# Attention scores from unsplit float32, each head of a pair in its own 64 rows of the array

## The chip, the cores and the metric

One core of a Trainium2 chip runs the whole program in one launch. The metric is the device time of that core in microseconds (us); smaller is better. TensorE (PE) multiplies matrices, and its weight loads (PEld) are shown as an engine of their own; VectorE is DVE, ScalarE is ACT, GpSimd is POOL, and SyncE (SP) issues all the transfers.

## The reference

Only the first part, the attention with its memory term, is touched. The two mixture and feed-forward parts behind it take the attention's output and stay as they are.

```python
B, H, S, D = (4, 8, 576, 64)          # q, k, v are (B, H, S, D) in float32
scores = (1 / np.sqrt(D)) * np.matmul(q, k.transpose(0, 1, 3, 2))
scores = np.where(np.triu(np.ones((S, S), bool), k=1), -1e9, scores)
a = np.exp(scores - scores.max(-1, keepdims=True))
a /= a.sum(-1, keepdims=True) + 1e-09
local = np.matmul(a, v)
...                                   # q_p = phi(q); mem_out = (q_p @ M_prev) / (q_p . z_prev)
out = g * mem_out + (1 - g) * local   # g = sigmoid(beta), one number for each head
```

## The kernel before

The 32 heads are worked in 16 pairs. A pair has 576 queries, cut into tiles t = 0 to 3 of 128 and a last tile of 64; in the last tile both heads share one array of 128 rows. Because of the causal mask, tile t needs 128(t + 1) keys and the last tile all 576, in two halves of 288 columns.

Scores are made from split numbers. `split` takes a head's queries and keys (both copies of them lie in the 128 partitions of `raw`) and writes the operands into one of three buffers R: part 0 writes the values rounded to the type float32r, part 1 the rests of the queries (in partitions 64 to 127), part 2 the rests of the keys. `scores` then multiplies twice over all 128 rows of the array, L361 with the keys' high parts and L362 with their rests, and adds up in PSUM. In the steady state the three parts run on POOL (L311, L331, L333). `scores_last` does the same for the last tile with four products for each half (L375, L376).

After a product, DVE scales it, adds the mask and finds the row's extreme (L363, or L378 for the last tile), and ACT takes the exponentials (L366, L384). The weights are transposed on PE (L401, L409) and copied to SBUF into PT by ACT or DVE (L251, L253), multiplied by the values (L454, L456, L461, the two heads in their own 64 columns of the array), transposed back (L477), combined with the memory term (L423 and L438) and transposed once more for the slots' logits (L501, L508, L515).

`step(p)` writes one pipeline step: scores of pair p + 1, transposes of pair p, values of pair p - 1, and the slots' softmax once in four pairs. Each piece has a position from the table T, the pieces are sorted by it, and that order is the priority in which a scheduler places the instructions in each engine's queue; an engine then runs its queue in order. Pieces of other work lie in the steps too: the decoding of the float64 weights `win` (ACT L230, DVE L233 to L236), the features of the memory term (L341, L345, L347), and one load of expert weights for each step.

PSUM has two banks for scores (pool pS), three for transposes (pT; combine, x_transposes and logits use it as well), and three others. PT exists once, the queries with values and memory (Q) twice. When attention ends, its buffers are filled with expert weights in the order of `places`: raw64, R2, raw, F, R0, R1, Q0, Q1, PT, M, P, x.

Of the kernel before, what the change touches and what calls it, by code (L numbers as in the profile page):

```python
# [8 lines left out]
F32 = mybir.dt.float32  # L9
# [17 lines left out]
# columns of the constants  # L27
# [6 lines left out]
# columns of the operands of the scores: 64 zeros, queries, 64 zeros, keys, keys' rests; the last 64  # L34
# queries come last for a pair's first head and first for its second
A_Q = 64
A_K1 = 704
A_K2 = A_K1 + S
A_END = A_K2 + S

# columns of a pair's second load: queries, values, memory with its norm
# [7 lines left out]
# a float64's high word read as a float32 grows with its size: at float32's smallest exponent, and  # L49
# at the largest value that float32 has  # L50
# [9 lines left out]
    load64=0.12317024323385276,  # L60
# [3 lines left out]
    val=[-0.023467514121727075, -0.010343477991731534, 0.01420002951651116, 0.08623092642954787, 0.17749026616632413],  # L64
    vout=0.1962084482935497,
# [19 lines left out]
    ps=0,  # L85
# [9 lines left out]
    s0=['a', 'm', 'p', 'v'],  # L95
# [11 lines left out]
ORDERS = [  # L107
# [8 lines left out]
]  # L116


CHOICES = {"NB": [3, 4], "sim": [0, 1]}
# [8 lines left out]
def tile_attention_moe_ffn(  # L128
# [37 lines left out]
    SIZE = {  # L166
        "raw": 2 * 2 * S, "R0": A_END, "R1": A_END, "R2": A_END, "P": 3200, "Q0": M_END, "Q1": M_END, "PT": 2 * 1984,
# [12 lines left out]
    # in the order they are used: 512 columns of w1 (expert group, row block, expert, half) and of w2  # L180
# [5 lines left out]
    def load_place(n, tag):  # L186
        """The next n units of weights, in a place of that many."""
# [78 lines left out]
    R = [place(f"R{i}", A_END, F32R) for i in range(3)]  # L266
# [25 lines left out]
    for i in range(3):  # L292
        POOL.memset(R[i][:, 0:64].bitcast(F32), 0.0)
        POOL.memset(R[i][:, 640:704].bitcast(F32), 0.0)
# [3 lines left out]
    raw_t, qvm_t, x_t, st_t, y_t, o_t, u_t = {}, {}, {}, {}, {}, {}, {}  # L298
# [16 lines left out]

    def split(p, h, part, eng=None):
        """Query and key rows as the high parts of their values, then the rests: the operands
        [q_hi; q_lo] and [k_hi; k_hi], [k_lo; k_lo]."""
        r, raw = R[(2 * p + h) % 3], raw_t[p, h]
        q = slice(A_Q, A_Q + S)  # L320
        if part == 0:
            dst = strided(r[:, A_Q:A_Q + 1], (A_K1 - A_Q, 2), (1, S))
            src = strided(raw[:, 0:1], (S, 2), (1, S))
            if eng in (None, "p"):
                pool_copy(dst, src)
            elif eng == "v":
                DVE.tensor_copy(dst, src)
            else:
                ACT.activation(out=dst, in_=src, func=AF.Copy)  # L329
        elif part == 1:  # L330
            (DVE if eng in ("a", "v", "m") else POOL).tensor_tensor(out=r[64:128, q], in0=raw[64:128, 0:S], in1=r[64:128, q], op=ALU.subtract)  # L331
        else:
            (DVE if eng in ("a", "v", "n") else POOL).tensor_tensor(out=r[:, A_K2:A_END], in0=raw[:, S:2 * S], in1=r[:, A_K1:A_K2], op=ALU.subtract)  # L333
            load_qk(p + 1, h)
# [14 lines left out]
    def stats(p):  # L349
        """0..7: sums (t, h), 8..17: norms (t, h), 18..25: minus the maxima, 26, 27: the last tile's."""  # L350
# [4 lines left out]
    def scores(p, h, t):  # L355
        r, st, pt = R[(2 * p + h) % 3], stats(p), Pt[h, t]
        n, c = 128 * (t + 1), 2 * t + h
        ps = pS.tile([128, 512], F32, tag="s", name="s")
        o = A_Q + 64 * h + t * 128
        a = r[:, o:o + 128]  # L360
# [248 lines left out]
    def step(p):  # L609
# [5 lines left out]
        if 1 <= p + 1 < NPAIR:  # L615
            add(T["rest"], load_rest, p + 1)
# [377 lines left out]
```

## Time and profile before

| | us |
|---|---|
| median of 3 runs | 591.15 |
| lowest, highest | 590.99, 593.15 |
| profiled execution, span from first to last instruction | 590.7 |
| PE busy in it | 548.4 (93%), with 3095 matmul instructions |
| DVE busy | 421.1 (71%) |
| ACT busy | 292.0 (49%) |
| POOL busy | 253.8 (43%) |

The profiled execution has only its span to show; the median of the runs lies 0.45 us above it, within their scatter. The span falls into the attention's start (to about 31 us), its steady steps (30.9 to 263.3), its end (to 290.5), the experts (to 345) and the last two layers (to 590.7). A matmul's row lasts from its start to the modelled end of its pipeline, so that rows overlap and a busy PE is not one at its peak: the pace of PE is read from the distance of successive rows.

### The profile page before, as it was taken

The numbers are of one execution on the slowest core, as the hardware profiler recorded it, in microseconds if no ns is written. First come the engines' busy times: TensorE is split into PE (matmuls) and PEld (weight loads), VectorE is DVE, ScalarE is ACT, GpSimd is POOL, SyncE is SP. The second block draws the span as 40 slices with busy tenths as digits, with TensorE's granted clock in tenths as the row PEclk, the third lists the DMA queues.
The fourth block names the chain that finished last, engine by engine and source line by source line (L and its number), as shares of the span: only waits on it lengthen the run. The fifth ranks groups of instructions, "written<-read, shape, count | busy, mean of one in ns | idle before, by whom it ended". The sixth has DMA issues, their size and how long they took to land.

```text
span 590.7 us, 9038 instructions
## 1 busy us (share of the span) xinstructions
PE 548.4 (93%) x3095; PEld 381.7 (65%) x3095; DVE 421.1 (71%) x978; ACT 292.0 (49%) x757; POOL 253.8 (43%) x234
## 2 busy tenths in 40 slices
PE   3899999989989999999999978878999999999997
PEld 2666665757646766666533235656888888888886
DVE  5889999998989999884324089997447557474670
ACT  4676767566656766663122065545463241423322
POOL 4486566763546667310000027899641140412302
PEclk9999999998989999999999999989999999999999
DMA  7667666543543545276899644240002010000101
GB/s 259 223 239 277 240 244 255 208 166 98 191 161 113 173 139 166 97 266 202 299 368 386 232 144 143 72 143 0 1 32 77 0 54 1 26 30 1 53 1 53
DMA packets 28957, 86.14 MB, mean 146 GB/s; under 512 B 3056, under 2 KB 3184, under 8 KB 28912
## 3 DMA queue, kind: packets, MB, share of 16 engines
q1 hardware_dynamic: 28912, 85.58, 40.8%
q8 instruction: 24, 0.39, 0.3%
q14 instruction: 21, 0.17, 0.1%
HBM read 80.85 MB, written 4.72 MB: 145 GB/s over the span
## 4 chain that ended last, share of the span: by engine, by line
PE 70%; DVE 17%; POOL 6%; issue 4%; ACT 2%; DMA 1%; SPq 0%; POOLq 0%; ACTq 0%; DVEq 0%
PE y L909 10%; PE y L907 10%; PE y L908 10%; PE t L401 5%; PE o L461 4%; PE y L770 3%; DVE P L363 3%; PE s L361 3%; POOL P L889 3%; PE o L456 3%; PE y L754 3%; PE h L878 2%; PE s L362 2%; POOL R L314 2%; PE y L423 2%
## 5 line engine op out<-in xcount | busy, mean ns | idle before, releaser
L909 PE MATMUL y<-w,R 128*128 128x512 f32 x288 | 115.5, 402 | 5.4 <-POOL R L314 5.4
L889 POOL TENSOR_SCALAR P<-P,sbt 128x384 f32<-128x384 f32 x31 | 34.8, 1122 | 198.3 <-ACT P L884 198.3
L907 PE MATMUL y<-w,R 128*128 128x512 f32 x288 | 115.6, 401 | 3.1 <-POOL R L311 2.9
L908 PE MATMUL y<-w,R 128*128 128x512 f32 x288 | 114.6, 398 | 1.4 <-DVE w L867 1.4
L882 ACT ACTIVATE P<-h 128x384 f32<-128x384 f32 x96 | 47.2, 491 | 121.6 <-PE h L878 121.3
L366 ACT ACTIVATE P<-P,st 128x128 f32<-128x128 f32 (+3 forms) x128 | 71.3, 559 | 32.6 <-DVE st L363 32.1
L893 DVE SCALAR_TENSOR_TENSOR P<-P,sbt 128x384 f32<-128x384 f32 x58 | 45.3, 781 | 56.1 <-ACT P L882 56.1
L363 DVE CUSTOM_DVE_ANT_0 P<-s,cs 128x128 f32<-128x128 f32 (+3 forms) x128 | 60.2, 481 | 13.7 <-PE s L362 13.5
L909 PEld LDWEIGHTS y<-w,R 128*128 128x128 f32 x288 | 55.0, 191 | 21.7 <-POOL R L314 8.3
L907 PEld LDWEIGHTS y<-w,R 128*128 128x128 f32 x288 | 55.1, 191 | 18.0 <-POOL R L311 5.6
L251 ACT ACTIVATE PT<-t 128x512 f32<-128x512 f32 (+3 forms) x144 | 55.9, 413 | 21.2 <-PE t L401 15.1
L908 PEld LDWEIGHTS y<-w,R 128*128 128x128 f32 x288 | 55.1, 191 | 11.4 <-DVE w L867 1.7
L361 PE MATMUL s<-R 128*128 128x128 f32 (+3 forms) x128 | 52.6, 413 | 10.3 <-DVE R L331 6.3
L401 PE MATMUL t<-cs,P 128*128 128x128 f32 x320 | 61.2, 296 | 0.2
L311 POOL TENSOR_SCALAR R<-raw 128x1152 fp32r<-128x1152 f32 x29 | 35.5, 1225 | 47.4 <-PE s L376 29.0
L401 PEld LDWEIGHTS t<-cs,P 128*128 128x128 f32 x320 | 38.4, 145 | 24.1 <-issue 13.1
L461 PE MATMUL o<-PT,Q 128*64 128x192 f32 (+3 forms) x256 | 52.0, 400 | 0.0
L333 POOL TENSOR_TENSOR R<-raw,R 128x576 fp32r<-128x576 f32 x30 | 45.8, 1528 | 8.8 <-ACT R L329 6.9
L331 POOL TENSOR_TENSOR R<-raw,R 64x576 fp32r<-64x576 f32 x29 | 45.1, 1556 | 2.4
L314 POOL TENSOR_TENSOR R<-P,R 128x384 fp32r<-128x384 f32 x38 | 44.3, 1165 | 3.2
L362 PE MATMUL s<-R 128*128 128x128 f32 (+3 forms) x128 | 43.1, 339 | 0.0
L895 DVE SCALAR_TENSOR_TENSOR R<-P,sbt,R 128x384 fp32r<-128x384 f32 x58 | 37.6, 649 | 5.4
(230 smaller groups left out, 1037.4 us busy)
## 6 DMA issues: line engine op xcount, KB each, us to landing
raw<-in_qk_dram SPq DMA_DIRECT2D x32, 576.0 KB, 3.7
Q<-in_qvm_dram SPq DMA_DIRECT2D x16, 673.0 KB, 5.0
w<-in_w_dram SPq DMA_DIRECT2D x19, 512.0 KB, 5.9
raw<-in_w_in_dram SPq DMA_DIRECT2D x8, 1024.0 KB, 5.7
w<-in_w_dram SPq DMA_DIRECT2D x32, 256.0 KB, 5.4
out_dram<-P SPq DMA_DIRECT2D x18, 256.0 KB, 2.1
raw<-in_w_out_dram SPq DMA_DIRECT2D x4, 1024.0 KB, 4.7
R<-in_w_dram SPq DMA_DIRECT2D x6, 512.0 KB, 6.1
```

What stands on the lines that cost most here:

```text
L251: ACT.activation(out=dst, in_=src, func=AF.Copy)
L314: POOL.tensor_tensor(out=dst, in0=a, in1=b, op=ALU.subtract)
L361: PE.matmul(ps[:, 0:n], a, r[:, A_K1:A_K1 + n], start=True, stop=False)
L362: PE.matmul(ps[:, 0:n], a, r[:, A_K2:A_K2 + n], start=False, stop=True)
L363: DVE.tensor_tensor_reduce(out=pt, in0=ps[:, 0:n], in1=cs[:, C_M2 - n:C_M2], scale=-0.125, scalar=BIG, op0=ALU.add, op1=ALU.min, accum_out ...
L366: ACT.activation(out=pt, in_=pt, func=AF.Exp, scale=-1.0, bias=st[:, 18 + c:19 + c], accum_out=st[:, c:c + 1])
L401: PE.transpose(tp[:, kb * 128:(kb + 1) * 128], Pt[h, t][:, kb * 128:(kb + 1) * 128], ident)
L461: last_pe[0] = PE.matmul(o[64 * h:64 * h + 64, q0 - 64:512], lhs(h), PT[p][0:rows, h, c:c + S - q0], start=False, stop=(kb == 4))
L889: POOL.tensor_scalar(out=r, in0=r, scalar1=sbt[:, 0:1], scalar2=sbt[:, 1:2], op0=ALU.mult, op1=ALU.add)
L907: PE.matmul(acc[g, i], hi[:, c], who[k], start=(k == 0), stop=False)
L908: PE.matmul(acc[g, i], hi[:, c], wlo[k], start=False, stop=False)
L909: PE.matmul(acc[g, i], lo[:, c], who[k], start=False, stop=(k == NK - 1))
```

## The change

Queries and keys are no longer split. A score is one float32 product over 64 rows of the array: the pair's first head uses rows 0 to 63, its second head rows 64 to 127, each with a PSUM bank of its own; in the last tile the two heads write the two halves of one bank. The keys are loaded alone (two loads of 64 partitions for each pair) into two halves of R1, the queries come from the pair's other load Q, of which there are now three (R2 is the third). `split` with its loads and the clearing of R is gone. PT exists twice (the second one in raw and R0). The tiles come in one order, 0, 1, last, 2, 3, each with transposes of both heads and then scores of both heads; the tables of offsets for them are gone. The values of a step have one position (0.05) instead of five. The pools change to three banks for scores and two for transposes (`ps=1`). Comments and docstrings are gone, and with them nothing that runs.

```diff
-    rest=0.695170733550659,
-    split=[-0.04277104398158898, 0.03196566297869962, 0.3161963354764645, 0.5106726172649579, 0.6789307619040896, 0.9898536413841046],
+    rest=0.35,
+    keys=0.02,
...
-    tpos=[-0.007428014231922566, -0.007428014231922566, -0.0017186653760416053, -0.007428014231922566, -0.007428014231922566, 0.2502093330615674, 0.0044618983662577764, -0.007428014231922566, -0.059387670387742744, -0.029043334600072676],
-    spos=[0.0023645466460246217, 0.0023645466460246217, 0.0023645466460246217, 0.14689391857384748, 0.0023645466460246217, -0.00397236720777216, 0.03582678126241105, 0.0023645466460246217, -0.0450101998423876, 0.0040102512909126285],
-    order=4,
...
-    val=[-0.023467514121727075, -0.010343477991731534, 0.01420002951651116, 0.08623092642954787, 0.17749026616632413],
-    vout=0.1962084482935497,
+    val=[0.05, 0.05, 0.05, 0.05, 0.05],
+    vout=0.08,
...
-    ps=0,
+    ps=1,
...
+ORDER = [0, 1, 4, 2, 3]
...
-    R = [place(f"R{i}", A_END, F32R) for i in range(3)]
+    KA = place("R1", SIZE["R1"])
...
-    PT = [place("PT", SIZE["PT"]).rearrange("p (h c) -> p h c", h=2)] * NPAIR
-    QA = [place(f"Q{i}", M_END) for i in range(2)]
-    raws = place("raw", SIZE["raw"])
+    PTA = place("PT", SIZE["PT"])
+    PT = [[PTA[:, 0:1984], PTA[:, 1984:3968]], [place("raw", SIZE["raw"])[:, 0:1984], place("R0", SIZE["R0"])[:, 0:1984]]]
+    QA = [place("Q0", M_END), place("Q1", M_END), place("R2", SIZE["R2"])[:, 0:M_END]]
...
-    def load_qk(p, h):
+    def load_keys(p):
         if p < NPAIR:
-            raw_t[p, h] = raws[:, 2 * S * h:2 * S * h + 2 * S]
-            SP.dma_start(out=raw_t[p, h], in_=qk[2 * p + h])
+            k_t[p] = KA[:, S * (p % 2):S * (p % 2) + S]
+            for h in range(2):
+                r = slice(64 * h, 64 * h + 64)
+                SP.dma_start(out=k_t[p][r, :], in_=qk[2 * p + h, r, S:2 * S])
...
-            qvm_t[p] = QA[p % 2]
+            qvm_t[p] = QA[p % 3]
...
-    def split(p, h, part, eng=None):
...
-        r, st, pt = R[(2 * p + h) % 3], stats(p), Pt[h, t]
+        st, pt, r = stats(p), Pt[h, t], slice(64 * h, 64 * h + 64)
...
-        PE.matmul(ps[:, 0:n], a, r[:, A_K1:A_K1 + n], start=True, stop=False)
-        PE.matmul(ps[:, 0:n], a, r[:, A_K2:A_K2 + n], start=False, stop=True)
+        PE.matmul(ps[:, 0:n], qvm_t[p][r, t * 128:(t + 1) * 128], k_t[p][r, 0:n], start=True, stop=True)
...
         for h in range(2):
-            r = R[(2 * p + h) % 3]
-            a = r[:, 0:128] if h else r[:, A_Q + 512:A_Q + 640]
-            k = 288 * g
-            PE.matmul(ps[:, 0:288], a, r[:, A_K1 + k:A_K1 + k + 288], start=(h == 0), stop=False)
-            PE.matmul(ps[:, 0:288], a, r[:, A_K2 + k:A_K2 + k + 288], start=False, stop=(h == 1))
+            r = slice(64 * h, 64 * h + 64)
+            PE.matmul(ps[r, 0:288], qvm_t[p][r, 512:S], k_t[p][r, k:k + 288], start=True, stop=True)
...
-        if 1 <= p + 1 < NPAIR:
-            add(T["rest"], load_rest, p + 1)
+        if p >= 0:
+            add(T["rest"], load_rest, p + 2)
+            add(T["keys"], load_keys, p + 2)
...
-        if 0 <= p + 2 < NPAIR:
-            for h in range(2):
-                for part in range(3):
-                    add(T["split"][3 * h + part], split, p + 2, h, part, T["s0"][2 + h] if p < 0 else None)
...
+        for t in ORDER:
             pos = acc / tot
...
+            acc += 6 if t == 4 else 2 * t + 2
             if 0 <= p < NPAIR:
...
+                if t == 4:
+                    add(T["scl"], scale_last, p)
+                for i in range(2):
+                    if t < 4:
+                        add(pos, transposes, p, i, t)
+                    else:
+                        add(pos, transposes_last, p, i)
             if 0 <= p + 1 < NPAIR:
...
+                for i in range(2):
+                    if t < 4:
+                        add(pos + 0.001, scores, p + 1, i, t)
+                    else:
+                        add(pos + 0.001, scores_last, p + 1, i)
...
-    load_qk(0, 0)
+    load_keys(0)
+    load_rest(0)
     SP.dma_start(out=cs, in_=cst)
-    load_qk(0, 1)
     SP.dma_start(out=bet, in_=beta)
-    load_rest(0)
+    load_keys(1)
+    load_rest(1)
...
-    for h in range(2):
-        for part in range(3):
-            split(0, h, part, T["s0"][h])
```

## Rows read from the trace of the kernel before

**Rows 1.** Busy time by stretch; the engines' columns are named in the first line
```profile
core 0: us, PE busy (x) PEld busy (x) DVE busy (x) ACT busy (x) POOL busy (x), PEclk, DMA share, GB/s
...
30.90:263.30 232.40, 220.33 (x1488) 148.98 (x1487) 214.04 (x602) 155.08 (x472) 133.28 (x101) 0.98 0.54 189
```

**Rows 2.** The chain of waits, 30.9 to 263.3 us, shares by line
```profile
by line: PE t L401 11.9%; PE o L461 7.5%; DVE P L363 6.4%; PE s L361 6.3%; PE o L456 5.4%; PE s L362 5.2%; PE y L423 4.8%; DVE win L235 4.1%; DVE F L347 3.6%; DVE win L234 3.4%; PE t L501 3.0%; DVE win L236 3.0%; DVE win L233 2.7%; issue 2.
```

**Rows 3.** PE in order of time, one step: start us, duration us, what
```profile
154.07 0.29 PE L375 MATMUL s<-R 128*128 128x288 f32 x1
...
154.21 0.30 PE L376 MATMUL s<-R 128*128 128x288 f32 x1
...
155.20 0.63 PE L501 MATMUL t<-cs,x 128*128 128x128 f32 x4 [0.43 <-DVE x L494]
...
155.76 0.27 PE L508 MATMUL t<-cs,x 64*128 64x64 f32 x1
...
155.96 0.66 PE L401 MATMUL t<-cs,P 128*128 128x128 f32 x4
...
156.69 0.40 PE L362 MATMUL s<-R 128*128 128x512 f32 x1
...
156.93 0.49 PE L401 MATMUL t<-cs,P 128*128 128x128 f32 x3
```

**Rows 4.** The same view, float32 products of the values
```profile
159.98 1.07 PE L456 MATMUL o<-PT,Q 128*64 128x512 f32 x2
...
161.42 0.64 PE L456 MATMUL o<-PT,Q 128*64 128x512 f32 x1
...
164.05 0.76 PE L461 MATMUL o<-PT,Q 128*64 128x320 f32 x4
```

**Rows 5.** Groups of POOL's instructions, 30.9 to 263.3 us: busy us, mean ns
```profile
L331 POOL TENSOR_TENSOR R<-raw,R 64x576 fp32r<-64x576 f32 x27 | 42.3, 1566 | 2.2
...
L311 POOL TENSOR_SCALAR R<-raw 128x1152 fp32r<-128x1152 f32 x26 | 32.1, 1233 | 46.4 <-PE s L376 29.0 <-PE s L362 17.4
```

**Rows 6.** DVE and POOL in order of time, in one step
```profile
162.95 1.15 POOL L311 TENSOR_SCALAR R<-raw 128x1152 fp32r<-128x1152 f32 x1 [3.64 <-PE s L362]
...
163.11 1.59 DVE L347 SCALAR_TENSOR_TENSOR F<-Q,F 128x576 f32<-128x576 f32 x1
```

**Rows 7.** Groups of DVE's instructions, 30.9 to 263.3 us: busy us, mean ns
```profile
L347 DVE SCALAR_TENSOR_TENSOR F<-Q,F 128x576 f32<-128x576 f32 x13 | 16.5, 1268 | 0.0
L235 DVE SCALAR_TENSOR_TENSOR win<-raw,win 128x512 int32<-128x512 int32 x16 | 16.1, 1007 | 0.0
L234 DVE TENSOR_SCALAR win<-win 128x512 int32<-128x512 int32 x16 | 15.6, 982 | 0.1
```

**Rows 8.** The same three lines: shortest, median and longest duration, ns
```profile
L347 DVE SCALAR_TENSOR_TENSOR F<-Q,F x13: 739/1234/1971, 48.7 to 248.9; 128x576 f32<-128x576 f32 x13
...
L235 DVE SCALAR_TENSOR_TENSOR win<-raw,win x16: 678/690/1920, 37.3 to 254.5; 128x512 int32<-128x512 int32 x16
...
L234 DVE TENSOR_SCALAR win<-win x16: 412/1028/1656, 35.4 to 253.8; 128x512 int32<-128x512 int32 x16
```

**Rows 9.** PE in order of time, the start of the program
```profile
6.33 0.79 PE L361 MATMUL s<-R 128*128 128x128 f32 x2 [6.33 <-DVE R L331]
...
14.35 0.44 PE L375 MATMUL s<-R 128*128 128x288 f32 x1
14.59 0.44 PE L376 MATMUL s<-R 128*128 128x288 f32 x1
...
20.07 0.28 PE L362 MATMUL s<-R 128*128 128x128 f32 x1
```

**Rows 10.** Groups of ACT's copies out of PSUM, 30.9 to 263.3 us: busy us, mean ns
```profile
L251 ACT ACTIVATE PT<-t 128x384 f32<-128x384 f32 x42 | 20.2, 482 | 6.7 <-PE t L401 4.3 <-PE t L409 2.3
```

**Rows 11.** SP and PE in order of time, the end of the attention
```profile
277.43 2.46 SPq L199 DMA_DIRECT2D PT<-in_w_dram  x4
...
290.54 1.92 PE L754 MATMUL y<-w,slT 128*32 128x512 f32 x16 [0.47 <-DVE slT L740]
```

More of the change, by code (lines that the diff above doesn't have):

```diff
@@ L32 @@
 C_END = C_REP + 128
[L36 to L39, printed above, removed]
+A_END = 1984
 M_V = S
@@ L94 @@
     dsum2=0.5750298499964066,
-    s0=['a', 'm', 'p', 'v'],
     cp=['pppddppppppqpqqq', 'dpdpppdpqdqddddq', 'pddpddddddddddpp'],
@@ L104 @@
 )
-ORDERS = [
[8 rows of a table removed]
-]
-CHOICES = {"NB": [3, 4], "sim": [0, 1]}
+ORDER = [0, 1, 4, 2, 3]
 def strided(ap, *dims):
@@ L166, in tile_attention_moe_ffn @@
     SIZE = {
-        "raw": 2 * 2 * S, "R0": A_END, "R1": A_END, "R2": A_END, "P": 3200, "Q0": M_END, "Q1": M_END, "PT": 2 * 1984,
+        "raw": 2 * 2 * S, "R0": A_END, "R1": 1856, "R2": 1856, "P": 3200, "Q0": M_END, "Q1": M_END, "PT": 2 * 1984,
         "raw64": 2048, "F": 1280, "x": 2560, "M": 1280}
@@ L291, in tile_attention_moe_ffn @@
         POOL.memset(FI[i][:, S:640], 0.0)
-    for i in range(3):
-        POOL.memset(R[i][:, 0:64].bitcast(F32), 0.0)
-        POOL.memset(R[i][:, 640:704].bitcast(F32), 0.0)
     POOL.memset(lT, NEG)
     POOL.memset(lgs, 0.0)
-    raw_t, qvm_t, x_t, st_t, y_t, o_t, u_t = {}, {}, {}, {}, {}, {}, {}
-    def load_qk(p, h):
+    k_t, qvm_t, x_t, st_t, y_t, o_t, u_t = {}, {}, {}, {}, {}, {}, {}
+    def load_keys(p):
         if p < NPAIR:
-            raw_t[p, h] = raws[:, 2 * S * h:2 * S * h + 2 * S]
-            SP.dma_start(out=raw_t[p, h], in_=qk[2 * p + h])
+            k_t[p] = KA[:, S * (p % 2):S * (p % 2) + S]
+            for h in range(2):
+                r = slice(64 * h, 64 * h + 64)
+                SP.dma_start(out=k_t[p][r, :], in_=qk[2 * p + h, r, S:2 * S])
     def load_rest(p):
         if p < NPAIR:
-            qvm_t[p] = QA[p % 2]
+            qvm_t[p] = QA[p % 3]
             SP.dma_start(out=qvm_t[p], in_=qvm[p])
@@ L314, in pool_sub @@
         POOL.tensor_tensor(out=dst, in0=a, in1=b, op=ALU.subtract)
-    def split(p, h, part, eng=None):
[L319 to L334, printed above, removed]
     def feature(p, part):
@@ L401, in transposes @@
             PE.transpose(tp[:, kb * 128:(kb + 1) * 128], Pt[h, t][:, kb * 128:(kb + 1) * 128], ident)
-        evac(strided(PT[p][:, h, 128 * t:128 * t + 1], (448, t + 1), (1, 128)),
+        evac(strided(PT[p % 2][h][:, 128 * t:128 * t + 1], (448, t + 1), (1, 128)),
              strided(tp[:, 0:1], (128, t + 1), (1, 128)), T["pt"][(4 * h + t) % len(T["pt"])])
@@ L409, in transposes_last @@
             PE.transpose(tp[:, i * 128:(i + 1) * 128], PL[:, (k0 + i) * 128:(k0 + i + 1) * 128], ident)
-        evac(strided(PT[p][:, 0, 448 * k0 + 512:448 * k0 + 513], (64 if k0 else 448, n), (1984, 2), (1, 64)),
-             strided(tp[:, 0:1], (128, n), (64, 2), (1, 64)), T["ptl"][part % len(T["ptl"])])
+        for h in range(2):
+            evac(strided(PT[p % 2][h][:, 448 * k0 + 512:448 * k0 + 513], (64 if k0 else 448, n), (1, 64)),
+                 strided(tp[:, 64 * h:64 * h + 1], (128, n), (1, 64)), T["ptl"][h])
     def memory(p, part):
@@ L453, in values @@
             for h in range(2):
-                PE.matmul(y[64 * h:64 * h + 64, 260:324], lhs(h), PT[p][:, h, 0:64], start=True, stop=True)
+                PE.matmul(y[64 * h:64 * h + 64, 260:324], lhs(h), PT[p % 2][h][:, 0:64], start=True, stop=True)
             for h in range(2):
-                PE.matmul(o[64 * h:64 * h + 64, :], lhs(h), PT[p][:, h, 64:576], start=True, stop=False)
+                PE.matmul(o[64 * h:64 * h + 64, :], lhs(h), PT[p % 2][h][:, 64:576], start=True, stop=False)
             return
@@ L460, in values @@
             c = 448 * kb + q0 if kb < 4 else 1920
-            last_pe[0] = PE.matmul(o[64 * h:64 * h + 64, q0 - 64:512], lhs(h), PT[p][0:rows, h, c:c + S - q0], start=False, stop=(kb == 4))
+            last_pe[0] = PE.matmul(o[64 * h:64 * h + 64, q0 - 64:512], lhs(h), PT[p % 2][h][0:rows, c:c + S - q0], start=False, stop=(kb == 4))
     def values_out(p):
@@ L626, in step @@
                 add(T["feat"][part], feature, p + 1, part)
-        order = ORDERS[T["order"]]
-        cost = [3 if h == 2 else t + 1 for h, t in order]
-        tot = float(sum(cost))
+        tot = float(sum(6 if t == 4 else 2 * t + 2 for t in ORDER))
         acc = 0.0
-        for n, ((h, t), c) in enumerate(zip(order, cost)):
+        for t in ORDER:
             pos = acc / tot
-            acc += c
+            acc += 6 if t == 4 else 2 * t + 2
             if 0 <= p < NPAIR:
-                if h < 2:
-                    add(pos + T["tpos"][n], transposes, p, h, t)
-                elif t == 0:
-                    add(pos + T["scl"], scale_last, p)
-                    add(pos + T["tpos"][n], transposes_last, p, 0)
-                    add(pos + T["tpos"][n], transposes_last, p, 1)
-            if 0 <= p + 1 < NPAIR:
-                if h < 2:
-                    add(pos + T["spos"][n] + 0.001, scores, p + 1, h, t)
-                else:
-                    add(pos + T["spos"][n] + 0.001, scores_last, p + 1, t)
+                if t == 4:
[5 more added lines that the diff above has]
+                        add(pos, transposes_last, p, i)
+            if 0 <= p + 1 < NPAIR:
+                for i in range(2):
[3 more added lines that the diff above has]
+                        add(pos + 0.001, scores_last, p + 1, i)
         for i in range(16):
@@ L820, in tile_attention_moe_ffn @@
     layer2(1)
-    RC = [place(f"R{i}", A_END, F32R) for i in range(3)]
+    RC = [place(f"R{i}", SIZE[f"R{i}"], F32R) for i in range(3)]
     ring = [RC[i][:, 1024 + TG * j:1024 + TG * j + TG] for i in range(2) for j in range(2)]
```

4 lines of the change are left out of this document (1 added, 3 removed), and 8 rows, old and new, of the table ORDERS.

## Prediction, before the result was known

> **What bounds the kernel now.** I read the table of stretches first, to find where the change can act: the steady steps of the attention take 232.4 us, which is 14 steps of 16.6 us, and there PE and DVE both look full (220 and 214 us) while POOL is at 133 [rows 1]. Neither number says which of them sets the step, so the chain of waits comes second [rows 2]. The lines listed there are PE's for 44% of the stretch (L401, L461, L361, L456, L362, L423, L501) and DVE's for 23% (L363, L235, L347, L234, L236, L233): two parts PE to one part DVE, and POOL has no line among them. Third I read PE in order of time for the pace of each kind of product, because a row's duration contains its pipeline and only the distance of rows is its cost [rows 3, 4]. Last I asked why a decode or a feature, which are SBUF work of fixed size, can take up to four times its shortest duration [rows 6 to 8].
>
> **The scores on PE.** A float32r product of 512 columns is followed by the next work 0.24 us later (156.69 to 156.93), one of 288 columns 0.14 us later, and 128 columns of a transpose cost 0.11 us (four in 0.63, a single one being 0.3) [rows 3]. At 0.47 ns a column 384 and 256 columns are 0.18 and 0.12; for 128 I take 0.11. Before, a pair needs four products of each width and eight of 288: 4 x (0.24 + 0.18 + 0.12 + 0.11) + 8 x 0.14 = 3.7 us. A float32 product stands as two instructions, and each costs 0.43 us for 512 columns (two in 1.07, one in 0.64 us), 0.84 ns a column [rows 4]. The pair's 1280 columns for each head and 576 of the last tile are then 1856 x 2 x 0.84 = 3.1 us if the two heads run side by side in their halves of the array, and 6.2 us if they run in turn. So this term lies between -0.6 and +2.5 us a step. No row shows two halves of rows side by side. The nearest are two halves of columns: four instructions of 320 columns, both heads of one key block, take 0.76 us [rows 4], where four of 0.27 in turn would take over 1.08. From that row I take side by side, -0.6.
>
> The Trainium skill, "TensorE: Matmul & The Clock Gate", section on packing small matmuls, says that products in different row groups run at once and gives 3.07 times for four of them. By it the sum is the one that I use; the trace agrees for columns alone.
>
> **Changes of the array's form.** Between the last of the four L501 (155.83) and L508, which uses 64 rows, and again until L401, which uses all 128, the ends lie 0.20 and 0.26 us apart where 64 and 128 columns cost 0.05 and 0.11 [rows 3]. A change of form costs 0.15 us. By the positions in T a step before has up to 14: five blocks of values among full-array work (10), L508 (2), logits (2). After, it has 17: five groups of scores (10), the values in one run (3), L508 and logits (4). That is +0.45 us. The one run of values also keeps the two heads of a key block together; in the step shown L456 runs 1.07 us for one head alone [rows 4]. I take half of one head's 0.86 us back, -0.4.
>
> PE's work thus changes by -0.6 + 0.45 - 0.4 = -0.55 us a step. Two thirds of it lie on the chain: 15 steps give -5 us.
>
> **POOL leaves, and DVE speeds up.** The split's three lines run on POOL in every step; two of them alone hold 74 us [rows 5], and the third is of like size. None is on the chain, but DVE pays for them: L347 starts at 163.11 behind L311 on POOL (162.95 to 164.10) and ends 0.60 us after it, so it takes 1.59 us for work of 0.74 [rows 6, 8]. From the means and the shortest times [rows 7, 8], with their shares of the chain [rows 2]: L347 8.4 us x (1 - 739/1268) = 3.5, L235 9.5 x (1 - 678/1007) = 3.1, L234 7.9 x (1 - 412/982) = 4.6, together 11 us. L236 and L233 hold another 13 us of the chain; at the same two ratios (0.33 and 0.58) they would give 6. The bounds are 0, if PE takes over every microsecond that DVE lets go, and -17. POOL keeps L394 and a few sums, so I take -12. What is late next is PE itself.
>
> **The start.** The first score waits until 6.33 us for a split, and the last one of pair 0 is at 20.07 [rows 9]. The 288-column products there stand 0.24 us apart, against 0.14 in the steady steps [rows 3]: PE has little more than half of its later pace. After, the scores wait for two loads of keys and one of queries. Pair 0 at that pace is 2 x 3.1 = 6.2 us of PE, so scores that begin at 5 or 6 can be over by 13. Not all of it counts, because the steps behind it fill up too: -5 us, bounds 0 (the mask or the queries land late) and -8.
>
> **Pairs that are torn apart.** Side by side needs both heads' products one behind the other in PE's queue. With three banks for two heads a second head may have to wait for DVE to free a bank, and the scheduler then puts other work between. A torn pair runs in turn, 1280 x 2 x 0.84 / 4 = 0.54 us more on average, and has two more changes of form, 0.3. Bounds: none torn, 0; all four of the step, 3.4 us. The order before keeps near to T's, with the scores a step's fraction late, so I take one pair in a step, a little less for slack: 0.6 x 15 = +9 us.
>
> **Costs of nothing.** The transfers shrink, and DMA stands at 0.54 in the stretch [rows 1]. Expert weights in raw and R0 must now wait for the last values; in return PT's half for even pairs comes free earlier. Loads into PT are issued at 277.43 and the first expert product is at 290.54 [rows 11]: these 13 us cover them. Without that cover the experts would start later by what is missing of it. The clearing of R and the split's rounding on ACT and DVE at the start are within the start's term.
>
> **The sum.** -5 - 12 - 5 + 9 = -13 us against the span of 590.7, so 577.7; the median of the runs shown lies 0.45 above the span: 578 us.
>
> **Rivals.** (B) The heads run in turn. For it: rows 4 show columns, not rows. Against it: nothing in the trace. PE's work rises by 3.1 us a step over the forecast; two thirds on the chain are +31 us, and of the 9 for torn pairs only the changes of form remain (+4): 578 + 31 - 5 = 604, slower. It decides from the point where more than about two pairs of a step run in turn (13 us of gain / 15 steps / 0.54 = 1.6 beyond those counted).
>
> (C) Only the last tile runs in turn, since its two heads write one bank of PSUM: 576 x 2 x 0.84 = 0.97 us a step, +14, 592 us. For and against it the trace has nothing but L461, whose two heads share a bank side by side with columns apart [rows 4]. The Trainium skill, "TensorEngine Tiling (Array Packing)", Gotcha 1, says that different row tiles cannot access the same PSUM bank at the same time; by that rule it is C, and no run here shows it.
>
> (D) Two banks for transposes are too few. Some 14 tiles of a step pass through them, and each is held until ACT has copied it, 0.48 us for 384 columns [rows 10]. If two transposes in each step wait for a copy in full, it is 1.0 us, +15, 593 us. For it: combine and logits hold a bank until DVE comes round. Against it: ACT is busy for 155 of 232 us [rows 1].
>
> (E) No pair is torn, DVE gives all of its 17 us, the start 8: 590.7 - 30 = 561.
>
> **How the numbers follow.** Forecast 0.45 (its own range 568 to 587), E 0.12, C 0.10, D 0.12, B 0.21. A change under 0.5% (588 to 594 us) is about what a measurement of this kernel cannot tell from none. Faster: forecast and E, 0.57. Same: C and half of D, 0.16. Slower: half of D and B, 0.27. The range runs from 556, below E, to 608, within B; outside it lie about half of B and a little of E.
>
> **What the next profile would show.** Right: score rows of two heads that start together, with the 64-row form; a 512-column pair that holds PE for about 0.86 us; POOL at a few tens of us; L347, L234 and L235 near their shortest times; the stretch of 14 steps near 219 us. Wrong: score instructions of the second head that start only when the first head's have streamed (B), last-tile rows alone in turn (C), PE waiting on ACT L251 or DVE copies out of the transposes' banks (D), or scores of one head with other work in between (torn).

## The result, and the profile after

The change made the kernel slower by a little: 595.56 us (median of 18 runs) against 592.15, a ratio of 1.0071 with a 95% interval of 1.0045 to 1.0096. The forecast was 578 us. The profiled execution of the changed kernel has a span of 591.9 us and took 594.05.

Two sizes moved by a lot and cancelled. The first stretch below is of the changed kernel, from 20 us to its first product of the experts (290.44 us); the columns are those of [rows 1].

```profile
core 0: us, PE busy (x) PEld busy (x) DVE busy (x) ACT busy (x) POOL busy (x), PEclk, DMA share, GB/s
20.00:290.40 270.40, 265.79 (x1710) 151.56 (x1709) 198.90 (x662) 169.64 (x529) 17.31 (x22) 1.00 0.42 141
```

The same stretch of the kernel before, to its first product of the experts (290.54 us):

```profile
20.00:290.50 270.50, 254.70 (x1725) 172.65 (x1725) 237.66 (x675) 170.09 (x518) 141.84 (x107) 0.98 0.55 194
```

The reader is to see that the attention ends at the same microsecond, 290.4 against 290.5, though POOL lost 124 us of work and VectorE 39. PE was free for 270.5 - 254.7 = 15.8 us before and for 4.6 after: 11.2 us of its waiting are gone, and its busy time grew by 11.1 us. What follows the first expert product takes 301.5 us after and 300.2 before; over the kernels below it takes 299.8 to 303.3, so that difference is not told from none.

VectorE did what was forecast. Its groups after, in the stretch of [rows 7]; L308 was L347, L215 was L235, L214 was L234:

```profile
L215 DVE SCALAR_TENSOR_TENSOR win<-raw,win 128x512 int32<-128x512 int32 x15 | 10.9, 724 | 0.0
L308 DVE SCALAR_TENSOR_TENSOR F<-Q,F 128x576 f32<-128x576 f32 x9 | 6.8, 756 | 0.5 <-ACT F L306 0.5
L214 DVE TENSOR_SCALAR win<-win 128x512 int32<-128x512 int32 x15 | 6.2, 417 | 0.0
```

The means fell from 1268, 1007 and 982 ns to 756, 724 and 417, close to the shortest of [rows 8]. On the page of the profile the chain of waits is now PE's, by engine and then by line:

```profile
PE 83%; POOL 6%; DMA 4%; issue 3%; DVE 2%; ACT 2%; SPq 0%; POOLq 0%; ACTq 0%; DVEq 0%
PE s L321 10%; PE y L860 10%; PE y L862 10%; PE y L861 10%; PE t L358 6%; PE o L419 5%; PE s L333 4%; PE y L723 3%; DMA raw<-in_w_in_dram 3%; PE y L707 3%; PE y L381 3%; POOL P L842 3%; PE h L831 2%; PE o L414 2%; POOL R L295 2%
```

The scores (L321) are on it. PE in order of time shows what became of them, as in [rows 3]; a float32 product is two instructions, so a pair of both heads is "x4" and one head alone "x2":

```profile
149.29 1.19 PE L333 MATMUL s<-R,Q 64*64 64x288 f32 x8
...
150.66 0.91 PE L321 MATMUL s<-R,Q 64*128 64x384 f32 x2
151.50 0.65 PE L435 MATMUL t<-cs,M 128*128 128x128 f32 x4
151.99 0.49 PE L358 MATMUL t<-cs,P 128*128 128x128 f32 x3
152.41 1.13 PE L321 MATMUL s<-R,Q 64*128 64x384 f32 x4
153.47 0.55 PE L358 MATMUL t<-cs,P 128*128 128x128 f32 x3
154.10 0.66 PE L459 MATMUL t<-cs,x 128*128 128x128 f32 x4
154.69 0.69 PE L321 MATMUL s<-R,Q 64*128 64x512 f32 x1
...
155.22 0.59 PE L321 MATMUL s<-R,Q 64*128 64x512 f32 x1
...
158.67 0.49 PE L321 MATMUL s<-R,Q 64*128 64x128 f32 x4
```

The 128-column pair at 158.67 stands together. The first head's 384 columns at 150.66 stand alone, with the transposes of `combine` and of tile 2 behind them. (The x4 at 152.41 is the second head's 384 columns and the first head's 512, two widths of two tiles.) The second head's 512 columns follow alone, from 154.69. Counted in the trace, 28 of the 64 pairs of L321 have other work between their heads, 12 of 384 and 14 of 512 columns among them: 1.8 a step, where the forecast took one. (The expectations below have 29, and 36 for E10, from a count made before the runs; the traces show 28 and 31.) Two of these rows run side by side all the same: 384 and 512 columns in turn would take (384 + 512) x 2 x 0.84 ns = 1.5 us, and the x4 takes 1.13. Five steps tear their wide pairs in this way and pay 512 columns once more, not 896.

The start went as told. Pair 0's scores begin at 6.06, as soon as its queries land, and end ahead of the first transposes at 14.96, where the kernel before had its last one at 20.07 [rows 9]:

```profile
6.06 1.62 PE L321 MATMUL s<-R,Q 64*128 64x128 f32 x6 [6.06 <-DMA Q<-in_qvm_dram]
...
11.47 3.55 PE L321 MATMUL s<-R,Q 64*128 64x384 f32 x8
14.96 0.44 PE L358 MATMUL t<-cs,P 128*128 128x128 f32 x2
```

### The profile page after: what moved, and what is told of

It reads as the page before. It is cut to its first block, busy times and chain, and to the rows that moved or that the text cites. A ratio compares the mean times of both kernels' runs of the same rounds, so it can differ in the third digit from the quotient of the medians.

```text
span 591.9 us, 8973 instructions
## 1 busy us (share of the span) xinstructions
PE 563.9 (95%) x3095; PEld 358.8 (61%) x3095; DVE 380.6 (64%) x979; ACT 292.4 (49%) x780; POOL 124.0 (21%) x140
## 4 chain that ended last, share of the span: by engine, by line
PE 83%; POOL 6%; DMA 4%; issue 3%; DVE 2%; ACT 2%; SPq 0%; POOLq 0%; ACTq 0%; DVEq 0%
PE s L321 10%; PE y L860 10%; PE y L862 10%; PE y L861 10%; PE t L358 6%; PE o L419 5%; PE s L333 4%; PE y L723 3%; DMA raw<-in_w_in_dram 3%; PE y L707 3%; PE y L381 3%; POOL P L842 3%; PE h L831 2%; PE o L414 2%; POOL R L295 2%
## 5 line engine op out<-in xcount | busy, mean ns | idle before, releaser
L325 ACT ACTIVATE P<-P,st 128x128 f32<-128x128 f32 (+3 forms) x128 | 71.3, 558 | 21.1 <-DVE st L322 18.9
L860 PEld LDWEIGHTS y<-w,R 128*128 128x128 f32 x288 | 55.1, 191 | 17.6 <-POOL R L292 5.6
L321 PE MATMUL s<-R,Q 64*128 64x128 f32 (+3 forms) x176 | 53.9, 503 | 6.6 <-DMA Q<-in_qvm_dram 6.1
L358 PE MATMUL t<-cs,P 128*128 128x128 f32 x320 | 53.5, 284 | 0.5 <-ACT M L229 0.3
L358 PEld LDWEIGHTS t<-cs,P 128*128 128x128 f32 x320 | 35.4, 141 | 27.3 <-ACT M L229 6.5
L351 POOL TENSOR_SCALAR P<-P,st 128x576 f32<-128x576 f32 x16 | 12.2, 762 | 138.9 <-DVE st L347 64.3
L831 PE MATMUL h<-x,R 128*128 128x384 f32 x96 | 34.6, 361 | 0.6 <-ACT P L835 0.6
L231 ACT ACTIVATE PT<-t 128x128 f32<-128x128 f32 (+4 forms) x88 | 28.7, 367 | 10.8 <-PE t L358 9.6
L847 DVE TENSOR_SCALAR R<-P,sbt 128x384 fp32r<-128x384 f32 x58 | 27.0, 465 | 5.9
L321 PEld LDWEIGHTS s<-R,Q 64*128 64x128 f32 x176 | 19.4, 196 | 17.1 <-issue 11.9
L231 ACT ACTIVATE raw<-t 128x128 f32<-128x128 f32 (+4 forms) x48 | 18.7, 389 | 18.0 <-PE t L358 10.2
```

The costliest lines, as they stand in the source:

```text
L321: PE.matmul(ps[:, 0:n], qvm_t[p][r, t * 128:(t + 1) * 128], k_t[p][r, 0:n], start=True, stop=True)
L325: ACT.activation(out=pt, in_=pt, func=AF.Exp, scale=-1.0, bias=st[:, 18 + c:19 + c], accum_out=st[:, c:c + 1])
L358: PE.transpose(tp[:, kb * 128:(kb + 1) * 128], Pt[h, t][:, kb * 128:(kb + 1) * 128], ident)
L831: PE.matmul(hp[:, 0:TG], G(k * 128, 128), cT[:, g * TG:(g + 1) * TG], start=True, stop=True)
L860: PE.matmul(acc[g, i], hi[:, c], who[k], start=(k == 0), stop=False)
```

## The experiments

Theory A: pairs that are torn apart make PE's work longer, by the array's time and by changes of form, and eat what VectorE's relief gives. Its rival R: the step is set by waits for VectorE, ACT and the banks, and PE's order matters only through them. The runs in one table. "Pair 2" is the time at which the third pair's first values start (L414, L456 before), "attention ends" the first product of the experts; PE's columns run from 20 us to there, as in the two rows above. A ratio is to the kernel before in the same session, with its 95% interval.

| kernel | median us | ratio | torn of 64 | pair 2 | attention ends | PE busy | PE free |
|---|---|---|---|---|---|---|---|
| before | 592.15 | 1 | | 61.65 | 290.5 | 254.7 | 15.8 |
| changed | 595.56 | 1.0071 (1.0045 to 1.0096) | 28 | 57.36 | 290.4 | 265.8 | 4.6 |
| E1 two score banks, three for transposes | 587.03 | none | 14 | 65.43 | 282.8 | 259.2 | 3.6 |
| E2 heads apart | 601.78 | 1.0162 (1.0103 to 1.0222) | 48 | 62.64 | 299.2 | 276.3 | 2.9 |
| E3 written order | 605.49 | 1.0229 (1.0163 to 1.0295) | 0 | 60.39 | 301.9 | 244.7 | 37.2 |
| E4 written order, banks of E1 | 585.05 | 0.9875 (0.9811 to 0.9939) | 0 | 57.36 | 278.8 | 242.8 | 16.0 |
| E5 pairs held, banks of E1 | 601.80 | 1.0186 (1.0111 to 1.0261) | 11 | 68.81 | 295.7 | 272.5 | 3.2 |
| E6 before, no splits | 574.36 | 0.9721 (0.9652 to 0.9790) | | 60.61 | 273.2 | 247.9 | 5.3 |
| E7 E4 with pairs torn | 618.00 | 1.0439 (1.0332 to 1.0546) | 60 | 70.83 | 318.3 | 290.6 | 7.7 |
| E8 E4, tuned | 577.70 | 0.9780 (0.9687 to 0.9873) | 0 | 59.24 | 272.4 | 235.3 | 17.1 |
| E9 changed, POOL's load back | 612.68 | 1.0362 (1.0313 to 1.0410) | 28 | 68.55 | 309.7 | 279.3 | 10.4 |
| E10 two banks each | 607.32 | 1.0285 (1.0235 to 1.0336) | 31 | 70.59 | 306.6 | 282.3 | 4.3 |
| E11 E4, tuned further | 568.07 | 0.9596 (0.9549 to 0.9643) | 0 | 65.08 | 267.2 | 238.9 | 8.3 |
| E12 before, banks of the change | 596.59 | 1.0061 (1.0026 to 1.0095) | | 62.40 | 292.6 | 256.1 | 16.5 |

PE's busy time holds waits that are shorter than a row, so it is not pure work; only kernels with the same products are compared by it. It also holds what the clock costs: the granted clock of that stretch is 1.00 in the changed kernel, E2, E6 and E10, and between 0.97 (E4) and 0.99 in the others.

The runs differ in the start as well, in how long PE goes at half its later pace [rows 9]. The same five transposes take 1.33 us early in E9 and 0.76 later:

```profile
26.12 1.33 PE L377 MATMUL t<-cs,P 128*128 128x128 f32 x5
...
42.53 0.76 PE L377 MATMUL t<-cs,P 128*128 128x128 f32 x5
```

The changed kernel has them (L366 there) at the later pace by 19.97 us:

```profile
19.97 0.77 PE L366 MATMUL t<-cs,P 128*128 128x128 f32 x5
```

Half the pace is what the lower of the clock's two levels gives, 1.2 against 2.4 GHz: in the kernel before, from 131.7 to 138.5 us, the granted clock is 0.50 and four transposes (L401) take 1.11 us at 134.87, against 0.66 at 155.96 [rows 3]. At the start the column of the granted clock does not show it; it stands at 1.00 from 0 to 20 us in both kernels. By such rows PE reaches its later pace at about 15 us in the changed kernel, 17 in E4, 29 in E1 and E7, 36 in E9 and 37 in E10. What decides this was not tried, and each kernel has one trace. In all of them it lies ahead of the time in the column "pair 2", so the stretch from there to the end of the attention compares the steps without it: 233.0 us in the changed kernel, 228.9 before.

**E1, the banks.** One line of the change undone, so that the transposes keep their third bank:

```diff
-    ps=1,
+    ps=0,
```

> The changed kernel with two banks for scores and three for transposes instead of three and two; nothing else. In the order of its instructions 14 of the 64 pairs of score products (128 to 512 columns) are torn, against 29 of 64 in the changed kernel. Theory A (torn pairs lengthen the step on PE): a torn pair of 384 or 512 columns costs 448 x 2 x 0.84 ns = 0.75 us of the array and two changes of form, 0.3 us; 15 pairs fewer are -16 us, so 576 to 584 us if nothing takes their place. Rival R (the step is set by DVE, ACT and the banks that they free, and PE's order only fills the time): within 4 us of the changed kernel, or slower, since the scores have one bank less.

The four times are 577.22, 586.99, 587.07 and 588.86, too scattered for an interval; the medians put it 0.9% below the kernel before and 1.6%, about 10 us, below the changed one. All four lie below the lowest of the changed kernel's 18 runs, 592.70 us, so the direction is shown and the size is not. In the profiled execution the steps from pair 2 on take 217.4 us against 233.0, 15.6 less, which is theory A's 16; the start gives half of it back, with pair 2 at 65.43 against 57.36. PE stays full to the end of the attention:

```profile
20.00:282.80 262.80, 259.23 (x1735) 151.55 (x1736) 200.18 (x688) 164.93 (x528) 18.52 (x22) 0.98 0.45 152
```

**E2, more pairs torn.** The positions of one head's pieces come ahead of the other's:

```diff
-                        add(pos, transposes, p, i, t)
+                        add(pos + 0.002 * i, transposes, p, i, t)
...
-                        add(pos + 0.001, scores, p + 1, i, t)
+                        add(pos + 0.001 + 0.002 * i, scores, p + 1, i, t)
```

> The changed kernel with the two heads of a tile one after the other in the order of the step: one head's transposes and scores, then the other's. 48 of the 64 pairs are torn, 19 more than in the changed kernel, about half of them narrow. Theory A: 19 x (about 0.35 us of the array + 0.3 us of changes of form) = +12 us, 604 to 612 us. Rival R: within 4 us of the changed kernel.

0.9% above the changed kernel, 5 us: half of what A gave, and beyond R's bound by a little. Of the 20 pairs that are newly torn 16 are of 128 and 256 columns, the cheap ones.

**E3 and E4, no pair torn.** Every matmul and transpose from `scores` to the slots' work is pinned behind the one written ahead of it (E4 with `ps=0` as well):

```diff
+    pin = tc.keep_in_program_order
...
-        PE.matmul(ps[:, 0:n], qvm_t[p][r, t * 128:(t + 1) * 128], k_t[p][r, 0:n], start=True, stop=True)
+        pin(PE.matmul(ps[:, 0:n], qvm_t[p][r, t * 128:(t + 1) * 128], k_t[p][r, 0:n], start=True, stop=True))
```

> The changed kernel with PE's instructions of the attention pinned to the order in which the step is written; the banks as in the changed kernel (three for scores, two for transposes). No pair is torn, and the last tile's four products stand together. Theory A: 29 pairs x 1.05 us = -30 us at most; PE can no longer go past an instruction that waits, so part of it comes back as waiting: 568 to 585 us. Rival R: PE's idle time rises by as much as its work falls or by more: 590 to 615 us.

> As the run in written order, with two banks for scores and three for transposes. Theory A: as that run, 568 to 585 us; the banks matter only through the order of PE, which is the same here, so the two lie within 5 us of each other. Rival R (banks and the engines that free them set the step): the two differ by more than 5 us, and neither is below 588 us.

E3 came out as R had it and E4 at the upper edge of A's range, and R's other mark is there too: they differ by 20 us, in nothing but the banks. Both free PE of 21 to 23 us of busy time. With two banks for transposes, 37.2 us come back as waiting, and the group of E3 that has most of it is the transposes; the last column is the idle time ahead and what ended it:

```profile
L359 PE MATMUL t<-cs,P 128*128 128x128 f32 x314 | 53.3, 288 | 20.6 <-ACT M L230 8.0 <-DVE M L234 3.8 <-DVE x L439 3.6
```

With three banks this group of E4 waits for 1.5 us:

```profile
L359 PE MATMUL t<-cs,P 128*128 128x128 f32 x314 | 50.3, 284 | 1.5 <-DVE M L234 0.8
```

I read the two theories as two faces of one shortage: where PE must keep the order, it waits for a bank; where the scheduler may go past the transposes, they come late and land between the heads of the next pair. The trace of the changed kernel fits: between the heads of all 28 torn pairs lie products that take a bank of the transposes, and in 10 of the 12 pairs of 384 columns they hold the three transposes of a head of tile 2, which are written ahead of both scores.

**E7, the price of a torn pair.** E4 with the positions of E2; pinned, so nothing else moves:

> The run in written order with two banks for scores, but in the order transposes of head 0, scores of head 0, transposes of head 1, scores of head 1: all 64 pairs are torn, nothing else differs. Theory A: a step gets (128 + 256 + 384 + 512) x 2 x 0.84 ns / 2 = 1.1 us of array work for each head's products that no longer run beside the other's, and 8 more changes of form, 1.2 us: 2.3 us a step, 15 steps +34 us, less what the 30 us of waiting in that run takes in: 600 to 619 us. Rival R (PE's order matters through its waits alone): within 6 us of that run, 579 to 591 us.

The 33 us lie at the top of A's range. Two things of the expectation were off. Pair 0's four pairs stay together, since no transposes lie between them yet, so 60 are torn. And its array term was halved by mistake: 1280 columns x 2 x 0.84 ns are 2.15 us a step, not 1.1. PE's busy time rose by 290.6 - 242.8 = 47.8 us, which is 0.80 us for a torn pair; the prediction had 0.54 + 0.3 = 0.84. PE's free time fell from 16.0 to 7.7 and took in part of it. Not all of the time is the steps': of the 39.5 us by which the attention ends later in the profiled execution, 13.5 lie ahead of pair 2 and 26.1 behind it. The 256-column tile of E4 and of E7, in order of time:

```profile
140.85 0.66 PE L359 MATMUL t<-cs,P 128*128 128x128 f32 x4
141.44 0.70 PE L322 MATMUL s<-R,Q 64*128 64x256 f32 x4
142.07 0.77 PE L367 MATMUL t<-cs,P 128*128 128x128 f32 x5
```

```profile
162.62 0.44 PE L359 MATMUL t<-cs,P 128*128 128x128 f32 x2
162.99 0.70 PE L322 MATMUL s<-R,Q 64*128 64x256 f32 x2
163.62 0.44 PE L359 MATMUL t<-cs,P 128*128 128x128 f32 x2
163.99 0.70 PE L322 MATMUL s<-R,Q 64*128 64x256 f32 x2
164.62 0.77 PE L367 MATMUL t<-cs,P 128*128 128x128 f32 x5
```

Both heads (x4) take 0.70 us together, and one head alone (x2) takes the same 0.70. From the first transpose to the next tile it is 1.22 us in E4 and 2.00 in E7.

**E5, pairs without pinning.** Two products of one column hold both banks, and the wide ones follow:

```diff
...
+        held = [PE.matmul(both[h][:, 0:1], qvm_t[p][r[h], q], k_t[p][r[h], 0:1], start=True, stop=True) for h in range(2)]
+        with tc.issue_after(held[0].ins), tc.issue_after(held[1].ins):
+            for h in range(2):
+                PE.matmul(both[h][:, 0:n], qvm_t[p][r[h], q], k_t[p][r[h], 0:n], start=True, stop=True)
...
```

> The run with two banks for scores, and in it each pair of score products is released together: a product of one column into each of the two banks first holds both, and the two wide products follow it (some 0.1 us a pair is added for that). 11 of 64 pairs are torn, against 14 with two banks alone and 29 in the changed kernel; PE may still go past what waits. Theory A (torn pairs lengthen the step on PE): near the run with two banks, 580 to 590 us, since only 3 pairs more stand together and the small products cost 64 x 0.1 = 6 us. If the waiting in the pinned orders, and not the pairs, made the difference between the pinned runs, this one shows the least waiting and the most gain: below 580 us.

Both expectations missed: 601.8 us, 15 above E1. Only 3 more pairs stand together, and PE is 13.3 us busier than in E1, twice what I gave the small products. How much of it is their own time and how much the order that they change was not taken apart. The run bears on neither theory.

**E6, VectorE's relief alone.** The kernel before without the splits from the third pair on. The scores of the later pairs are computed from the first pairs' operands, so what is left out is their own queries and keys:

```diff
+        if p >= 2:
+            if part == 2:
+                load_qk(p + 1, h)
+            return
         if part == 0:
```

> The kernel before, without the splitting of queries and keys from the third pair on: the scores of pairs 2 to 15 are computed from the operands of the first two pairs, which stay in place, so the output is not the reference's; the loads stay. It leaves PE's work and order as before and takes away POOL's and some of DVE's hold-up. Theory: VectorE's operations behind POOL's splits were on the path for about 12 us (bounds 0 and 17), so 575 to 582 us. Rival: PE takes over every microsecond that VectorE lets go, 588 to 593 us.

It gives 2.8%, 16.5 us (17.6 by the medians): the upper bound of the term, and no sign that PE takes it over. Nearly all of it, 16.3 us, lies behind pair 2 (212.6 us against 228.9):

```profile
20.00:273.20 253.20, 247.89 (x1731) 171.56 (x1730) 199.04 (x679) 170.86 (x522) 19.87 (x23) 1.00 0.59 207
```

**E9, the relief taken back.** The changed kernel with POOL's work of the old splits on a scratch that nothing reads:

```diff
+    def pool_load(p, part):
+        a = qvm_t[p]
+        if part == 0:
+            pool_copy(scr[:, 0:576], a[:, 0:576])
+            pool_copy(scr[:, 0:576], a[:, 576:1152])
+        elif part == 1:
+            pool_sub(scr[64:128, 0:576], a[64:128, 0:576], a[64:128, 576:1152])
+        else:
+            pool_sub(scr[:, 0:576], a[:, 0:576], a[:, 576:1152])
...
+        if 0 <= p < NPAIR - 2:
+            for i in range(6):
+                add((-0.0428, 0.032, 0.3162, 0.5107, 0.6789, 0.9899)[i], pool_load, p, i % 3)
```

> The changed kernel with POOL's load of the kernel before put back: in every step, at the places of the old splits, two copies of 576 columns and two subtractions (64 and 128 rows) for each head into a scratch that nothing reads. If the relief of VectorE counts in the changed kernel as much as the run without splits showed in the kernel before (17.6 us), 608 to 615 us. If PE's own work now sets the step and VectorE has slack behind it (PE waits for only about 10 us of its 15 steps), the load costs little: 594 to 602 us.

The time is in the first range: 1.0362 against 1.0071 is 2.9%, 17 us, as much as E6. That the two agree is in part luck. Of the 19.3 us by which the attention ends later in the profiled execution, 11.2 lie ahead of pair 2, where PE stays at half its pace until about 36 us; the steps behind it take 241.2 us against 233.0, 8.2 more, half of E6's 16.3. Nor is VectorE the only way for the load to cost time: POOL's own sums now stand behind it in POOL's queue, and PE waits 3.8 us for one of them:

```profile
L470 PE MATMUL t<-cs,x 128*128 128x128 f32 x64 | 10.7, 284 | 5.9 <-POOL x L464 3.8 <-DVE x L459 1.1 <-DVE x L463 0.6
```

So the load costs time in the steps too, although the chain of the changed kernel is 83% PE's; how much of the 8.2 us is VectorE's was not taken apart. Two of VectorE's groups in E9, whose lines were L216 (682 ns) and L308 in the changed kernel:

```profile
L216 DVE SCALAR_TENSOR_TENSOR win<-raw,win 128x512 int32<-128x512 int32 x16 | 16.3, 1018 | 0.1
L319 DVE SCALAR_TENSOR_TENSOR F<-Q,F 128x576 f32<-128x576 f32 x10 | 10.0, 996 | 0.5 <-ACT F L317 0.3
```

**E10, which bank it is.** E1 gave back a bank to the transposes and took one from the scores; this run takes the one and does not give the other (`ps=2`: two for scores, two for transposes, two for the values' sums).

```diff
-    ps=1,
+    ps=2,
```

> The changed kernel with two banks for scores, two for transposes and two for the values' sums, where the run with two banks for scores also had three for transposes. 36 of 64 pairs are torn in its order. If the third bank of scores tears the pairs by letting the heads drift apart, this one gains like the run with two banks, 584 to 590 us. If it is the missing third bank of transposes (the scheduler goes past a transpose that finds no bank, and puts the next thing between the two scores), nothing is gained: 594 us or more, 7 pairs x 1 us above the changed kernel at most, 594 to 604 us.

607.32 us, 12 above the changed kernel and 20 above E1, with 31 pairs torn: the second case, and 3 us beyond its range. It is the third bank of the transposes that counts: from pair 2 on, E1 takes 217.4 us and E10 236.0. A third bank for scores does not tear pairs. What E10 loses to the changed kernel it loses for the most part at the start, with pair 2 at 70.59 us against 57.36; from there on it takes 3.0 us more:

```profile
20.00:306.60 286.60, 282.26 (x1731) 162.49 (x1730) 201.36 (x679) 172.08 (x537) 18.57 (x22) 1.00 0.40 135
```

**E12, the same bank without halves of rows.** The kernel before with the line of the change:

```diff
-    ps=0,
+    ps=1,
```

> The kernel before with the change's banks alone: three for scores and two for transposes in place of two and three. Its score products use all the rows of the array, so the order of two heads' products costs nothing there. If the missing third bank of transposes costs time through the pairs that it tears, it does not cost here: 588 to 596 us. If it costs by itself, through waits for the copies out of the banks, whatever the form of the scores, 598 to 612 us.

It falls between the two: 0.6%, 3.6 us. Where no order of two heads costs anything, the move of the bank costs this; in the changed kernel it costs about 10 (E1, without an interval). This fits a bank that hurts by itself and more so through the pairs; E1 is too scattered to fix the second part.

**E8 and E11, the order filled.** From E4 on, with the waits of PE that it shows given other work. E8 leaves the slots' dispatch unpinned, puts `xt` behind the widest transposes and the values behind the second tile's scores:

```diff
-    val=[0.05, 0.05, 0.05, 0.05, 0.05],
-    vout=0.08,
+    val=[0.079, 0.079, 0.079, 0.079, 0.079],
+    vout=0.1,
...
-    xt=0.5523273520209158,
+    xt=0.6926,
```

> The run in written order with two banks for scores, with three waits of PE in it taken away by places in the order: the slots' dispatch products of every fourth step are not pinned (6.6 us of waiting for ACT there), the transposes of x go behind the transposes of the widest tile (3.4 us of waiting for VectorE), and the values go behind the second tile's scores (1.5 us). No pair is torn. If PE sets the step, the time falls by these 7 to 11 us: 574 to 578 us. Rival: another engine or a load is late next and gives it back: 582 to 588 us.

The time is as expected, its reason is not: the dispatch transposes still wait 7.4 us for ACT, and the 64-row transpose of x now waits 5.8, so PE's free time did not fall (16.0 to 17.1). Its busy time did, by 7.5 us. The 64-row transpose of x now stands directly ahead of the widest tile's scores, which use 64 rows as well; that saves two changes of form a step, 15 x 2 x 0.15 = 4.5 us by the prediction's price; the rest is not assigned.

E11 moves the dispatch as well and parts the transposes of x:

```diff
-    dT=-0.04697371816400439,
-    dsum=0.2294730404353726,
+    dT=0.0785,
+    dsum=0.24,
...
-            add(T["xt"], x_transposes, v)
+            add(T["xt"] - 0.0006, x_transposes, v, 1)
+            add(T["xt"], x_transposes, v, 0)
```

> The tuned run in written order, with its two largest waits of PE filled: the slots' dispatch transposes wait 7.4 us for ACT and go behind the second tile's scores; the 64-row transpose of x waits 5.8 us for a bank and goes ahead of the widest tile's transposes. No pair is torn. If PE sets the step, 10 us less than the tuned run: 564 to 570 us. If VectorE, ACT or the loads of the float64 weights are late next: 572 to 579 us.

568.07 us, 4% below the kernel before (0.9549 to 0.9643) and the fastest of all, with PE free for 8.3 us:

```profile
20.00:267.20 247.20, 238.89 (x1731) 146.71 (x1732) 193.75 (x678) 164.75 (x535) 18.38 (x22) 0.99 0.47 157
```

## Why the prediction was wrong

**VectorE's relief, -12 (bounds 0 and -17).** Right in kind, and it stands at its bound: 16.5 us by E6. E9's 17 us are no second measure of it, since most of them arise at the start.

**PE's work, -5.** The mechanism held: two heads in their halves of rows take the time of one (0.70 us in E4 and E7), so rival B is refuted. The last tile runs side by side too, eight instructions of 288 columns in 1.19 us at 149.29, where eight in turn would be 8 x 288 x 0.84 ns = 1.94: rival C is refuted. The size of the gain was not measured by itself; the nearest is E4, with no pair torn, whose PE is busy for 5.1 us less than in E6, at a lower granted clock (0.97 against 1.00), where the forecast had 15 x 0.55 = 8 us on PE.

**The start, -5.** The scores of pair 0 end some 5 us earlier, as forecast, and pair 2 is reached 4.3 us earlier (57.36 against 61.65). What this is worth at the end was not tried. One sign was summed wrongly: "the stretch of 14 steps near 219 us" takes the start's 5 us out of a stretch that does not hold the start.

**Torn pairs, +9.** This is the step that failed, "I take one pair in a step, a little less for slack". The price was right for the mean of the four widths, 0.84 us on PE against 0.80 in E7. The count and the widths were not: 28 pairs, not 15, and 26 of the 28 have 384 or 512 columns. Less the five that run beside another tile, they are 12 x 384 + 14 x 512 + 2 x 256 - 5 x 384 = 10368 more columns and 23 more groups of scores; by the prediction's own prices that is 17.4 + 6.9, an estimate of 24 us on PE, where the sum had 9. PE bears it out: the changed kernel's is busy for 21.1 us more than E3's, with the same products, the same banks and no torn pair, and for 23.0 more than E4's. In time, all that is not VectorE's came to -1 in the sum (-5, -5, +9) and to 1.0071 - 0.9721 = 3.5%, 21 us, on the chip (the changed kernel against E6). The 15 us of torn pairs beyond the forecast make most of these 22 us; the rest is not assigned to single edits.

**Why the count was wrong.** The prediction looked for the cause at the scores' three banks, where a second head might have to wait for VectorE. E10 shows the other side: with two banks for scores and still two for transposes as many are torn (31). The transposes lost a bank in the change; with it given back (E1) 14 pairs are torn, about the one in a step that the prediction took, and why those are torn was not tried. The prediction had the missing bank as rival D, a wait of PE of 15 us with a chance of 0.12, beside the torn pairs and not as their cause. D's mark in the profile, PE waiting for the copies out of the transposes' banks, is missing after (4.6 us free in all), as I read it because the order is made ahead of the run and takes something else in place of the wait. Pinned, the wait shows itself (E3, 20.6 us ahead of the transposes). D's 593 us lay near the result with the right bank and the wrong form. E12's 3.6 us are what the bank costs where no pair can be torn.

**The weights at the end, 0.** Right: the first expert product waits 0.38 us, for the slots and not for a load.

```profile
290.44 1.88 PE L707 MATMUL y<-w,slT 128*32 128x512 f32 x8 [0.38 <-DVE slT L693]
```

The forecast's 578 us are there to be had: E8 reaches them and E11 passes them, with the same products and no pair torn, but also with other pieces of the step moved.

## What to carry to other kernels

When two products gain only if they are neighbours in an engine's queue, count the pairs that are neighbours in the order that the program really has, and do not estimate it: here the mean price of a torn pair was right to 5%, the count was off by nearly two, and the pairs that were torn were the wide ones. A bank taken from one stage need not show as a wait of that stage; a scheduler goes past it, and the cost turns up as longer work elsewhere, which pinning the order makes visible again. A chain of waits that is 83% one engine's does not say that the others have slack: putting POOL's load back cost 17 us, 8 of them in the steady steps. And before two runs are compared by their ends, see where in the program the difference arises: 11 of the 19 us of E9's trace lie at its start, where PE was still at half its pace.

## What the runs showed of the hardware

Two row halves that write two halves of the partitions of one PSUM bank ran side by side: 1.19 us for the eight instructions at 149.29, against 1.94 in turn. The Trainium skill, "TensorEngine Tiling (Array Packing)", Gotcha 1, says that they cannot access one bank at the same time; here the measurement differs, and it decides.

POOL's work of about 125 us on a scratch that nothing reads slowed operations of VectorE by a third to a half (L308 and L216): L216 went from 682 to 1018 ns in the mean. The Trainium skill, "SBUF — State Buffer", section "Who interferes with whom", has one exclusive lock between the two for an operation of VectorE with two inputs in SBUF; L216, which reads raw and win, agrees with it. What this alone costs the kernel E9 does not tell.

Up to 15 us in one kernel and 37 in another PE goes at half its later pace (five transposes 1.33 us against 0.76 in E9), while the column of the granted clock stands at 1.00.
